# One pool of six PSUM banks in the attention stage: coarse counts move into it

## The chip, the cores and the metric

The kernel runs on one core of a Trainium2 chip. The metric is the device time of one execution in microseconds (us). TensorE (PE in the profile, its weight loads PEld), VectorE (DVE), ScalarE (ACT), GpSimd (POOL) and SyncE (SP) run side by side, each in its own order, and wait for one another through semaphores. PSUM, into which TensorE writes, has eight banks of 512 fp32 columns over 128 partitions.

## The reference, cut to what matters

```python
# attention: 8 batches, 8 heads, 576 positions, 64 wide
scores = q @ k.T / 8            # heads 0-3: the last 32 positions; heads 4-7: each fourth of the last 128
attn = exp(scores - max) / (sum + 1e-9)
x = (attn @ v) as (4608, 512)   # tokens x model width
# routing: capacity 576 tokens for each of 8 experts
logits = x @ w_gate             # (4608, 8)
for idx in argsort(-logits.flatten()):      # greedy, best pair first
    if token free and counts[expert] < 576: assign
out[tokens of e] = relu(x[tokens of e] @ w1[e]) @ w2[e]
```

## The kernel before, in words

There are two stages, attention and mixture of experts. **Attention** works in 32 units (four per batch: two kinds of head, two units each). A unit computes 36 score products into the two banks `pm` (`scores`, L398), takes masked maxima on DVE out of them (`most`, L403), subtracts them on POOL (`shift`, L409), transposes the result in three groups into banks `pS` (`turn`, L416), takes exponentials on ACT (`exps`, L412, planned at 400 ns each), multiplies by the values into banks `px` in two groups of 20 and 16 products (`values`, L424), and divides by the sums on ACT and DVE (`sums` L428, `weigh` L433 and L434). After each second unit the result is transposed in three groups into `px` (`banks`, L475) and copied out (ACT, or DVE for two of the three groups of the last units, L482). After a batch the gate's logits follow: `by_expert` and `by_token` (L516, L548), or for the last batch `narrow` (L540), whose bank is held until all parts are in; DVE copies them to `Lt` (L566).

`Router.choose` then finds for each token its best expert, key and flags (`keys` L763 to L768, `choices` L773). `coarse` compares each token's key with 256 steps (L647), one chunk of 128 tokens at a time, and `coarse_counts` (L652) counts, by two narrow products per chunk, how many tokens of each expert lie above each step. The counts of all 36 chunks add up in one bank, `pz`, which the Router owns for the whole kernel. When attention has ended, `search_alone` turns them into flags (L725), a first product (L728) and four finer rounds of comparisons and counts; the list of the first expert's tokens follows, and the experts' products, which are the second stage (`moe`).

Eight banks are given out in attention: two `pm`, two `pS`, three `px` (the third first serves as target of zero products, `keep_clock`, L119, until the 17th PE operation of the list is placed), one `pz`.

The order of instructions is written by a **planner** (`Schedule`). Each operation has an engine, an estimated cost, dependencies and a due time: the planned end less the longest path behind it, less a boost. An operation that names a `Buf` gets a bank of its pool when it is placed, the one that comes free earliest by the planner's own estimates, and the bank is held until all its users are placed. A change of the product's form on PE (`whole`, `half`, `quarter`, `narrow`) is charged. The coarse operations of the first seven batches carry a boost of -105500 ns: they are due far behind all else and go where an engine would stand idle. Once placed, each engine's order is fixed, and on the chip an engine waits for what its next instruction needs. SP issues the loads in the order in which the planner placed them.

Of the kernel before, what the change touches and what calls it, by code (L numbers as in the profile page):

```python
# [32 lines left out]
NK = 16  # L33
NM = 5
FE = 400
F0, F1 = 6, 17
PARTS = (5, 15, 16)
OB = (12, 12, 12), (6,) * 6
TOL_DVE, TOL_ACT, TOL_POOL, TOL_PE, T_W = 100, -50, 200, 500, 730
# [205 lines left out]
def attention(tc, ctx, C, load_const, T, xd, Lt, R):  # L245
# [21 lines left out]
    wgp = pk.tile([128, 4, 32], F32, name="wgp")  # L267
    LT = ring(pk, [128, S], F32, "lt", 2)
    banks_ = lambda n, k: [ps.tile([128, 512], F32, name=f"{n}{i}") for i in range(k)]
    PM, PS, PV = Pool([banks_("pm", 2)]), Pool(banks_("pS", 2)), Pool(banks_("px", 3))  # L270
    act = lambda o, i: nc.scalar.activation(o, i, AF.Copy)  # L271

    users = {}
# [182 lines left out]
    def banks(un, xs, done, usex):  # L456
# [36 lines left out]
            return  # L493
        tokens(un)

    def coarse(c0, c1, x, late):
        for c in range(c0, c1):
            g, used, use_ = PRE.take()
            f = op("DVE", 290, lambda c=c, g=g: R.coarse(c, g), [x, *used], late)
            counted[0] = op("PE", 60, lambda c=c, g=g: R.coarse_counts(c, g), [f, ready["c", 3], counted[0]], late,  # L500
                            form="whole")
            use_.append(counted[0])

    lt_ = {}

# [21 lines left out]
    def tokens(un):  # L527

        b, u = un.b, un.u
        c0, c1 = b * S // 128, (b * S + S) // 128  # L530
        late = B_K if b < B - 1 else B_E
        n = c1 - c0
        last = b == B - 1

        def narrow(gs):
            for c in range(c0, c1):
                for g in gs:
                    for p in range(0, 128, 32):
# [12 lines left out]
        if last:  # L551
            pt = Buf(PV)
            before = [*xt_[b - 1]]
            t = un.op("PE", 140 * n, lambda: narrow([0, 1]), [*before, *xt_[b][:3], ready["w"]], late, pt, "narrow")
            t = un.op("PE", 140 * n, lambda: narrow([2, 3]), [t, *xt_[b]], late, None, "narrow")
            for of in (b - 1, b):
                for kk in range(2):
                    xt_[of, kk][2].append(t)
        else:
            by_expert(un, late)  # L560
            pt = Buf(PV)
            of = [lt_[x] for x in (b - 1, b) if x >= 0]
            t = un.op("PE", 125 * n, by_token, [*(k for x in of for k in x[1]), ready["c", 3]], late, pt, "half")
            for x in of:
                x[2].append(t)
        k = un.op("DVE", 150, lambda: nc.vector.tensor_copy(  # L566
            Lt[:, c0:c1], pt.tile[:, :NE * n].rearrange("p (c e) -> p c e", e=NE)), [t], late)
        pt.users.append(k)
        x = un.op("DVE", 1000, lambda: R.choose(c0, c1), [k], late)
        coarse(c0, c1, x, B_P if not last else late - u * P_U)  # L570


    counted = [None]
    fill, warm = PV.tiles[2], R.zero
    PV.held[2] = Buf(PV)
    keep_clock(nc, warm, fill, F0)
    cold = [True]

    def idle(x, gap):
        if x.eng == "PE" and cold[0]:  # L580
            if x in PV.held[2].users:
                cold[0] = False
            elif x.n > first_pe[0]:
                keep_clock(nc, warm, fill, int(max(0, gap - 400) / 430))

    op("DVE", 300, lambda: nc.vector.memset(R.pz[:, :256], 0.0), (), B_P)
    load(0, 0, 0)
    const(0)
    const(1)
# [20 lines left out]
        Unit(u).build()  # L610
    pe = [x for x in K.ops if x.eng == "PE"]
    first_pe = [pe[0].n]
    PV.held[2].users.append(pe[F1])
    K.run(idle)


class Router:


    def __init__(self, tc, ctx, C, Lt):  # L620
        nc = tc.nc
        self.tc, self.C = tc, C
        self.pf = ctx.enter_context(tc.tile_pool(name="r_fix", bufs=1))
        self.Lt = Lt
        self.A = self.pf.tile([128, NCH], F32, name="A")
        self.PR = self.pf.tile([128, 32], F32, name="PR")
        self.M = self.pf.tile([128, NCH], F32, name="M")
        self.V0 = self.pf.tile([128, NCH], F32, name="V0")
        self.oh0 = self.pf.tile([128, NCH, NE], BF, name="oh0")
        self.key0 = self.pf.tile([128, NCH], I32, name="key0")  # L630
        self.bits = self.pf.tile([128, NCH], I32, name="bits")
        self.bt = self.pf.tile([128, 5, NE], F32, name="bt")
        self.zero = self.pf.tile([128, 512], BF, name="zero")
        self.pz = ctx.enter_context(tc.tile_pool(name="r_ps", bufs=1, space=PSUM)).tile([128, 512], F32, name="pz")
        self.open = self.pf.tile([128, NE], F32, name="open")
        nc.vector.memset(self.zero, 0.0)
        nc.gpsimd.memset(self.open, 1.0)
        nc.gpsimd.memset(self.A, 0.0)
        nc.gpsimd.memset(self.PR, 0.0)

    def work(self, ctx):
# [7 lines left out]
    def coarse_counts(self, c, g):  # L649
        nc = self.tc.nc  # L650
        for h in range(2):
            nc.tensor.matmul(self.pz[:, 400 + NE * h:400 + NE * h + NE], g[:, 128 * h:128 * h + 128], self.oh0[:, c],  # L652
                             start=(c == 0 and h == 0), stop=(c == NCH - 1), skip_group_check=True)

    def counts(self):

# [60 lines left out]
    def search_alone(self, V, oh, last):  # L717
# [1 line left out]
        nc, C, pw = self.tc.nc, self.C, self.pw  # L719
        psc = self.pa[:, :1]  # L720
        if not last:
            junk = pw.tile([128, 2, NE], F32, name="junkc")
            flag = pw.tile([128, 2], BF, name="flagc")
            for h in range(2):
                nc.vector.tensor_scalar(junk[:, h], self.pz[:, 400 + NE * h:400 + NE * h + NE], float(CAP), None,  # L725
                                        op0=OP.is_ge, op1=OP.max, accum_out=flag[:, h:h + 1])
            for h in range(2):
                nc.tensor.matmul(psc, C["unit1"], flag[:, h:h + 1], start=(h == 0), stop=(h == 1))  # L728
# [31 lines left out]
    def keys(self, c0, c1, M, key, V):  # L760

        nc = self.tc.nc
        nc.vector.tensor_reduce(M, self.Lt[:, c0:c1], axis=AX.X, op=OP.max)  # L763
# [7 lines left out]
    def choices(self, c0, c1, M, oh):  # L771

        self.tc.nc.vector.tensor_tensor(oh, self.Lt[:, c0:c1], M[:, :, None].to_broadcast([128, c1 - c0, NE]),  # L773
                                        op=OP.is_equal)

    def choose(self, c0, c1):

        sl = slice(c0, c1)
        self.keys(c0, c1, self.M[:, sl], self.key0[:, sl], self.V0[:, sl])
        self.choices(c0, c1, self.M[:, sl], self.oh0[:, sl])  # L780
        if c1 < NCH:
            self.marks(c0, c1)

# [136 lines left out]
    def close(self):  # L920
# [6 lines left out]
        self.keys(0, NCH, self.M, key, self.V)  # L927

    def ranks(self):
        nc, C = self.tc.nc, self.C  # L930
# [33 lines left out]
    def leave(self):  # L964

        nc, pw = self.tc.nc, self.pw
        Mo = pw.tile([128, NCH], F32, name="Mo")
        self.oh = pw.tile([128, NCH, NE], BF, name="oh")
        self.assign()
        nc.vector.scalar_tensor_tensor(Mo, self.A, -3e38, self.M, op0=OP.mult, op1=OP.add)  # L970
        self.choices(0, NCH, Mo, self.oh)

    def start(self):
        self.flags(self.V, None, self.kstep(0, False))
# [66 lines left out]
def moe(tc, ctx, C, R, xd, w1, w2, out):  # L1041
    nc = tc.nc
    ps = ctx.enter_context(tc.tile_pool(name="m_ps", bufs=1, space=PSUM))
    pw = ctx.enter_context(tc.tile_pool(name="m_w", bufs=1))
    R.work(ctx)
    ctx.enter_context(tc.manual_schedule())
    NF, ND = FF // 128, DM // 128
    CUT = (0, 256, CAP)
# [15 lines left out]
    HB = ring(pw, [128, 2 * CAP + 64], F32R, "hb", NF + 1)  # L1064
    Y = ring(pw, [128, DM], F32, "y", 3)
    R.pa, fill = PYR.tiles[1], PHR[0].tiles[1]


    R.alone()
# [401 lines left out]
```

## Time and profile before

| | us |
|---|---|
| median of 3 runs | 652.55 (651.42 to 652.75) |
| profiled execution | 648.04 |
| span in its trace (first to last instruction) | 646.20 |
| attention proper, tail, routing (see below) | 10 to 150, 150 to 160, 160 to 190 |

The profiled execution is 1.84 us longer than its span. Where the profile gives an instruction's duration, a run of matmuls in one line is `xN`; a matmul's end is modelled, so distances from start to start are the surer reading. Lines are those of the kernel before. The brackets at the end of a line of the timeline tell how long the engine stood idle before and what ended that.

### The profile page before, as it was taken

What the parts mean: (1) busy time and instruction counts of PE and PEld (TensorE: products, weight loads), DVE (VectorE), ACT (ScalarE), POOL (GpSimd) and SP (SyncE); (2) the same over time, 40 slices, a digit from 0 to 9 for tenths busy, and PEclk for the clock granted to TensorE, in tenths of its full rate; (3) what the DMA queues carried; (4) which work ended last, traced back from release to release, by engine and by line L of the source; (5) the groups of instructions that cost most, each with busy time, mean ns of one, the idle gap of its engine ahead of it and who ended that gap; (6) DMA issues with size and microseconds to landing.
All of it is one profiled execution on the core that took longest, in us unless ns stands there. A gap on an engine that the chain in (4) does not pass through costs nothing.

```text
span 646.2 us, 17963 instructions
## 1 busy us (share of the span) xinstructions
PE 615.7 (95%) x6749; PEld 530.2 (82%) x6749; DVE 451.1 (70%) x1930; ACT 304.8 (47%) x691; POOL 195.4 (30%) x326
## 2 busy tenths in 40 slices
PE   8999999997569999999999999999999999999994
PEld 5887888786439978977998898799889879989983
DVE  3768678875787888994998699699879736615200
ACT  3868788753037345853453425345343345325210
POOL 3434433331053156544006103400610520431011
PEclk9999999998569999999999999999999999999998
DMA  8999999823049468991155217115423743211010
GB/s 318 391 294 281 308 281 291 224 61 75 3 141 255 73 162 289 196 317 57 58 182 156 69 40 256 71 49 182 154 69 107 245 164 127 70 54 58 1 42 32
DMA packets 62680, 100.18 MB, mean 155 GB/s; under 512 B 7280, under 2 KB 26224, under 8 KB 62592
## 3 DMA queue, kind: packets, MB, share of 16 engines
q1 hardware_dynamic: 53216, 73.82, 35.4%
q0 software_dynamic: 9376, 25.21, 14.8%
q8 instruction: 53, 0.87, 0.5%
q14 instruction: 35, 0.29, 0.1%
HBM read 73.83 MB, written 18.87 MB: 143 GB/s over the span
## 4 chain that ended last, share of the span: by engine, by line
PE 75%; issue 11%; DVE 5%; POOL 2%; DMA 2%; ACT 2%; SPq 1%; POOLq 0%; DVEq 0%; ACTq 0%
PE ph L1285 26%; PE py L1327 19%; PE px L424 5%; PE pS L416 5%; PE pm L398 5%; PE px L475 2%; PE pz L660 2%; PE py L1330 2%; PE py L1332 2%; POOL out L1353 1%; DMA raw<-in_moe_w 1%; PE ph L1254 1%; PE px L516 1%; ACT vo L271 1%; PE ph L119 1%
## 5 line engine op out<-in xcount | busy, mean ns | idle before, releaser
L1327 PE MATMUL py<-w2h,hb 128*128 128x512 f32 x512 | 164.7, 394 | 0.0
L1285 PE MATMUL ph<-xh,w1h 128*128 128x256 f32 (+1 forms) x512 | 138.6, 301 | 0.0
L1285 PE MATMUL ph<-xh,w1l 128*128 128x256 f32 (+1 forms) x512 | 136.4, 297 | 0.0
L1285 PE MATMUL ph<-xl,w1h 128*128 128x256 f32 (+1 forms) x512 | 135.9, 296 | 0.0
L1327 PEld LDWEIGHTS py<-w2h,hb 128*128 128x128 f32 x512 | 96.1, 188 | 19.8
L1071 ACT ACTIVATE hb<-ph 128x256 fp32r<-128x256 f32 (+2 forms) x192 | 59.8, 346 | 105.4 <-PE ph L1285 101.6
L1327 PE MATMUL py<-w2l,hb 128*128 128x512 f32 x256 | 99.8, 390 | 0.0
L1285 PEld LDWEIGHTS ph<-xh,w1h 128*128 128x128 f32 x512 | 91.5, 189 | 0.7 <-issue 0.3
L1285 PEld LDWEIGHTS ph<-xl,w1h 128*128 128x128 f32 x512 | 91.5, 189 | 0.1
L1285 PEld LDWEIGHTS ph<-xh,w1l 128*128 128x128 f32 x512 | 91.5, 190 | 0.0
L1353 POOL DMA_INDIRECT out<-y,tok x40 | 40.2, 1006 | 147.0 <-ACT y L1071 67.4
L409 POOL TENSOR_TENSOR sc<-sc,mx 128x480 f32<-128x480 f32 x64 | 56.9, 910 | 89.6 <-DVE mx L403 89.6
L1071 ACT ACTIVATE y<-py 128x512 f32<-128x512 f32 (+1 forms) x40 | 23.9, 597 | 126.8 <-PE py L1327 100.5
L1305 DVE SCALAR_TENSOR_TENSOR hb<-ph,hb 128x320 fp32r<-128x320 f32 (+1 forms) x128 | 57.3, 452 | 28.8 <-ACT hb L1071 27.7
L403 DVE CUSTOM_DVE_ANT_0 sc<-pm,const 128x96 f32<-128x96 f32 x288 | 53.8, 253 | 22.6 <-PE pm L398 19.9
L1199 POOL DMA_INDIRECT xg<-xd,idx x40 | 42.6, 1066 | 53.3 <-issue 34.9
L1327 PEld LDWEIGHTS py<-w2l,hb 128*128 128x128 f32 x256 | 48.1, 188 | 9.1
L412 ACT ACTIVATE et<-pS 96x384 f32<-96x384 f32 x96 | 43.2, 485 | 24.4 <-PE pS L416 23.8
L1072 DVE TENSOR_TENSOR w2l<-raw,w2h 128x512 fp32r<-128x512 f32 x48 | 31.5, 684 | 20.2 <-ACT w2h L1071 19.9
L416 PE MATMUL pS<-const,sc 128*96 128x128 f32 x288 | 43.9, 281 | 0.9 <-ACT et L412 0.9
L1071 ACT ACTIVATE w1h<-raw 128x512 fp32r<-128x512 f32 x64 | 37.6, 627 | 6.6 <-DMA raw<-in_moe_w 6.6
L398 PE MATMUL pm<-k,q 64*64 64x96 f32 x1152 | 36.9, 257 | 1.8 <-DVE mx L403 0.6
(188 smaller groups left out, 982.3 us busy)
## 6 DMA issues: line engine op xcount, KB each, us to landing
raw<-in_moe_w SPq DMA_DIRECT2D x128, 256.0 KB, 4.5
k<-in_kp SPq DMA_DIRECT2D x16, 304.0 KB, 6.1
k<-in_kd SPq DMA_DIRECT2D x16, 304.0 KB, 6.3
q<-in_qp SPq DMA_DIRECT2D x16, 288.0 KB, 5.4
q<-in_qd SPq DMA_DIRECT2D x16, 288.0 KB, 6.3
xd<-xs SPq DMA_DIRECT2D x64, 72.0 KB, 3.2
xd<-xs SPq DMA_DIRECT2D x16, 288.0 KB, 6.7
w2l<-raw POOLq DMA_DIRECT2D x16, 256.0 KB, 5.2
```

What stands on the lines that cost most here:

```text
L398: nc.tensor.matmul(o[w:w + 64], self.Q[c][r:r + 64], self.K[c][r:r + 64], start=True, stop=True)
L403: nc.vector.tensor_tensor_reduce(out=sc[:, c], in0=pms[g][:, c // 2 * KB:c // 2 * KB + KB], in1=mm[:, c if self.kind else min(1, c)], scal ...
L409: nc.gpsimd.tensor_tensor(sc[:, g::2], sc[:, g::2], mx[:, g::2, None].to_broadcast([128, n, KB]), op=OP.subtract)
L412: nc.scalar.activation(self.E0[:, 384 * j:384 * j + 384], pt[:KB, :384], AF.Exp, scale=-1.0)
L416: nc.tensor.transpose(pt[:KB, 128 * x:128 * x + 128], sc[:, ORD[3 * j + x]], C["identf"])
L424: nc.tensor.matmul(px[64 * a:64 * a + 64, x - c0], self.E0[:, w:w + 64], self.V[c][a], start=True, stop=True)
L1071: act = lambda o, i, f=AF.Copy: nc.scalar.activation(o, i, f)
L1199: nc.gpsimd.indirect_dma_start(out=xg[:n], out_offset=None, in_=xd, in_offset=bass.IndirectOffsetOnAxis(ap=box[0][:n, m:m + 1], axis=0))
L1285: nc.tensor.matmul(o, a[:, d * 128:d * 128 + 128], b[:, d, c0:c1], start=((d, i) == pairs[0]), stop=((d, i) == pairs[-1]))
L1305: hl = op("DVE", 335 if j == 0 else 400, lambda: nc.vector.scalar_tensor_tensor(hb[:, CAP + c0:CAP + c1], o, 0.0, hb[:, c0:c1], op0=OP.max ...
L1327: nc.tensor.matmul(py, x, w, start=(f + i == 0), stop=(f == NF - 1 and i == 2))
L1353: s = nc.gpsimd.indirect_dma_start(out=out, out_offset=bass.IndirectOffsetOnAxis(ap=box[1][:n, m:m + 1], axis=0), in_=y[:n], in_offset=None)
```

## The change

- `pS`, `px` and the Router's `pz` give up their own banks: attention now has two `pm` banks and one pool of six (`PV`, also named `PS`). The sixth serves the zero products at first, until the same 17th PE operation.
- Coarse counts of a batch take a bank of that pool. For the first seven batches all chunks of a batch are one PE operation, which starts the bank anew, and a DVE addition (`coarse_sum`) adds the 16 columns to a table `cc` in SBUF. For the last batch, an identity product first puts `cc` into the bank (`coarse_sum_of`), the chunks' counts add to it one by one as before, and DVE reads the flags out of it at once (`coarse_flags`); `search_alone` uses these.
- In the last batch `choose` reads the logits out of their bank, and ACT copies them to `Lt` beside it; in the other batches DVE copies them first, as before.
- `pz` is taken from the second stage's banks; its zeroing moves from DVE at the start to ACT at the beginning of the second stage.
- One more zero product at the start: seven in place of six.

```diff
-F0, F1 = 6, 17
+F0, F1 = 7, 17
-    PM, PS, PV = Pool([banks_("pm", 2)]), Pool(banks_("pS", 2)), Pool(banks_("px", 3))
+    PM, PV = Pool([banks_("pm", 2)]), Pool(banks_("px", 6))
+    PS = PV
...
     def coarse(c0, c1, x, late):
+        gs, pt, last = [], Buf(PV), c1 == NCH
         for c in range(c0, c1):
             g, used, use_ = PRE.take()
             f = op("DVE", 290, lambda c=c, g=g: R.coarse(c, g), [x, *used], late)
-            counted[0] = op("PE", 60, lambda c=c, g=g: R.coarse_counts(c, g), [f, ready["c", 3], counted[0]], late,
-                            form="whole")
-            use_.append(counted[0])
+            gs.append((c, g, f, use_))
+        k = None
+        if last:
+            k = op("PE", 60, lambda: R.coarse_sum_of(pt.tile), summed[-1:], late, buf=pt, form="whole")
+        for part in [[y] for y in gs] if last else [gs]:
+            def count(part=part):
+                for c, g, *_ in part:
+                    R.coarse_counts(c, g, pt.tile, c == c0 and not last, c == c1 - 1)
+
+            k = op("PE", 10 + 50 * len(part), count, [*(y[2] for y in part), ready["c", 3], k], late,
+                   buf=None if k else pt, form="whole")
+            for y in part:
+                y[3].append(k)
+        f = R.coarse_flags if last else R.coarse_sum
+        summed.append(op("DVE", 200, lambda: f(pt.tile), [k], late))
+        pt.users.append(summed[-1])
...
-        k = un.op("DVE", 150, lambda: nc.vector.tensor_copy(
-            Lt[:, c0:c1], pt.tile[:, :NE * n].rearrange("p (c e) -> p c e", e=NE)), [t], late)
-        pt.users.append(k)
-        x = un.op("DVE", 1000, lambda: R.choose(c0, c1), [k], late)
+        if last:
+            x = un.op("DVE", 1000, lambda: R.choose(of_bank(pt), c0, c1), [t], late)
+            pt.users += [x, un.op("ACT", 250, keep, [t], late)]
+        else:
+            k = un.op("DVE", 150, keep, [t], late)
+            pt.users.append(k)
+            x = un.op("DVE", 1000, lambda: R.choose(Lt[:, c0:c1], c0, c1), [k], late)
         coarse(c0, c1, x, B_P if not last else late - u * P_U)
...
-    op("DVE", 300, lambda: nc.vector.memset(R.pz[:, :256], 0.0), (), B_P)
...
+    def coarse_sum(self, pt):
+        o = self.cc.rearrange("p h e -> p (h e)")
+        self.tc.nc.vector.tensor_tensor(o, o, pt[:, :2 * NE], op=OP.add)
+    def coarse_sum_of(self, pt):
+        self.tc.nc.tensor.matmul(pt[:, :2 * NE], self.C["identf"], self.cc.rearrange("p h e -> p (h e)"), start=True,
+                                 stop=False, skip_group_check=True)
+    def coarse_flags(self, pt):
+        for h in range(2):
+            self.tc.nc.vector.tensor_scalar(self.cj[:, h], pt[:, NE * h:NE * h + NE], float(CAP), None,
+                                            op0=OP.is_ge, op1=OP.max, accum_out=self.cf[:, h:h + 1])
...
+    nc.scalar.activation(R.pz[:, :256], R.zero[:, :256], AF.Copy)
```

## Rows read from the trace of the kernel before

**Rows 1.** The page: TensorE's share, and its granted clock in 40 slices

```profile
PE 615.7 (95%) x6749; PEld 530.2 (82%) x6749; DVE 451.1 (70%) x1930; ACT 304.8 (47%) x691; POOL 195.4 (30%) x326
...
PEclk9999999998569999999999999999999999999998
```

**Rows 2.** Stretches: length, then busy us of each engine, clock, DMA share, GB/s

```profile
10.00:150.00 140.00, 137.46 (x2966) 113.40 (x2964) 105.57 (x764) 106.34 (x244) 55.14 (x62) 1.00 0.86 268
150.00:160.00 10.00, 6.38 (x159) 5.08 (x158) 4.94 (x20) 2.55 (x8) 0.00 (x0) 0.87 0.28 62
160.00:190.00 30.00, 17.80 (x276) 11.49 (x277) 23.62 (x97) 3.44 (x6) 6.26 (x9) 0.53 0.17 51
```

**Rows 3.** Waits of TensorE, 9 to 150 us: total us, times, longest us

```profile
PE pS L416 <- ACT et L412: 0.6, 2, 0.4
PE pm L398 <- DVE mx L403: 0.6, 2, 0.3
```

**Rows 4.** The chain that ended last, 15 to 25 us: start, us, what

```profile
17.46 1.20 PE px L424 x36
...
19.53 0.73 PE px L424 x20
...
22.15 0.62 PE px L424 x16
```

**Rows 5.** Timeline of the tail: start, us, engine, line, operation [idle before]

```profile
147.95 0.86 PE L540 MATMUL px<-wgp,xt 128*32 128x8 f32 x80
...
151.62 0.87 ACT L412 ACTIVATE et<-pS 96x384 f32<-96x384 f32 x2 [0.43 <-PE pS L416]
...
152.16 0.53 PE L416 MATMUL pS<-const,sc 128*96 128x128 f32 x3 [0.31 <-ACT et L412]
...
152.62 0.80 PE L424 MATMUL px<-v,et 96*64 96x65 f32 x20
...
155.22 0.84 PE L475 MATMUL px<-const,xs 128*128 128x128 f32 x6 [1.33 <-DVE xs L434]
155.78 1.02 DVE L482 COPY xt<-px 128x384 f32<-128x384 f32 x2 [0.70 <-PE px L475]
...
156.39 0.55 PE L475 MATMUL px<-const,xs 128*128 128x128 f32 x3 [0.32 <-DVE xt L482]
...
156.98 0.49 ACT L271 ACTIVATE xt<-px 128x384 f32<-128x384 f32 x1 [2.86 <-PE px L475]
...
158.81 0.20 DVE L566 COPY Lt<-px 128x40 f32<-128x40 f32 x1 [2.00 <-PE px L540]
159.04 0.20 DVE L763 TENSOR_REDUCE M<-Lt 128x5 f32<-128x40 f32 x1
...
160.22 1.00 PE L652 MATMUL pz<-oh,pre 128*128 128x8 bf16 x10 [1.46 <-DVE pre L647]
...
179.85 0.60 ACT L992 ACTIVATE rx<-oa,const 128x360 bf16<-128x360 bf16 x1 [22.38 <-DVE oa L983]
```

**Rows 6.** Timeline: first and last counts before the tail; an addition out of PSUM

```profile
63.43 0.20 PE L652 MATMUL pz<-oh,pre 128*128 128x8 bf16 x2
...
150.89 0.26 PE L652 MATMUL pz<-oh,pre 128*128 128x8 bf16 x4
...
183.67 0.17 DVE L1013 TENSOR_TENSOR t<-t,ptx 64x20 f32<-64x20 f32 x1
```

**Rows 7.** Timeline of TensorE in the first 14 us

```profile
1.20 2.74 PE L119 MATMUL px<-zero 128*128 128x512 bf16 x6 [1.20 <-DVE zero L636]
4.48 1.86 PE L398 MATMUL pm<-k,q 64*64 64x96 f32 x36 [0.54 <-DMA k<-in_kp]
...
7.74 1.95 PE L398 MATMUL pm<-k,q 64*64 64x96 f32 x36
...
12.72 1.04 PE L398 MATMUL pm<-k,q 64*64 64x96 f32 x36
```

**Rows 8.** Groups by line, 0 to 158 us: count, busy us, mean ns, idle before

```profile
L412 ACT ACTIVATE et<-pS 96x384 f32<-96x384 f32 x96 | 43.2, 485 | 24.4 <-PE pS L416 23.8
```

More of the change, by code (lines that the diff above doesn't have):

```diff
@@ L494, in banks @@
         tokens(un)
+    summed = []
     def coarse(c0, c1, x, late):
+        gs, pt, last = [], Buf(PV), c1 == NCH
         for c in range(c0, c1):
@@ L565, in tokens, with keep, of_bank @@
                 x[2].append(t)
-        k = un.op("DVE", 150, lambda: nc.vector.tensor_copy(
-            Lt[:, c0:c1], pt.tile[:, :NE * n].rearrange("p (c e) -> p c e", e=NE)), [t], late)
-        pt.users.append(k)
-        x = un.op("DVE", 1000, lambda: R.choose(c0, c1), [k], late)
+        def keep():
+            (act if last else nc.vector.tensor_copy)(Lt[:, c0:c1], of_bank(pt))
+        def of_bank(pt):
+            return pt.tile[:, :NE * n].rearrange("p (c e) -> p c e", e=NE)
+        if last:
[5 more added lines that the diff above has]
+            x = un.op("DVE", 1000, lambda: R.choose(Lt[:, c0:c1], c0, c1), [k], late)
         coarse(c0, c1, x, B_P if not last else late - u * P_U)
-    counted = [None]
-    fill, warm = PV.tiles[2], R.zero
-    PV.held[2] = Buf(PV)
+    fill, warm = PV.tiles[5], R.zero
+    PV.held[5] = Buf(PV)
     keep_clock(nc, warm, fill, F0)
@@ L580, in idle @@
         if x.eng == "PE" and cold[0]:
-            if x in PV.held[2].users:
+            if x in PV.held[5].users:
                 cold[0] = False
@@ L612, in attention @@
     first_pe = [pe[0].n]
-    PV.held[2].users.append(pe[F1])
+    PV.held[5].users.append(pe[F1])
     K.run(idle)
@@ L633, in __init__ @@
         self.zero = self.pf.tile([128, 512], BF, name="zero")
-        self.pz = ctx.enter_context(tc.tile_pool(name="r_ps", bufs=1, space=PSUM)).tile([128, 512], F32, name="pz")
+        self.cc, self.cj = (self.pf.tile([128, 2, NE], F32, name="c" + x) for x in "cj")
+        self.cf = self.pf.tile([128, 2], BF, name="cf")
         self.open = self.pf.tile([128, NE], F32, name="open")
@@ L638, in __init__, with work @@
         nc.gpsimd.memset(self.A, 0.0)
+        nc.gpsimd.memset(self.cc, 0.0)
         nc.gpsimd.memset(self.PR, 0.0)
-    def work(self, ctx):
+    def work(self, ctx, ps):
+        self.pz = ps.tile([128, 512], F32, name="pz")
         self.pw = ctx.enter_context(self.tc.tile_pool(name="r_work", bufs=2))
@@ L647, in coarse, with coarse_counts @@
         self.tc.nc.vector.tensor_scalar(g, self.C["coarse"], self.V0[:, c:c + 1], None, op0=OP.is_le)
-    def coarse_counts(self, c, g):
-        nc = self.tc.nc
+    def coarse_counts(self, c, g, pt, start, stop):
         for h in range(2):
-            nc.tensor.matmul(self.pz[:, 400 + NE * h:400 + NE * h + NE], g[:, 128 * h:128 * h + 128], self.oh0[:, c],
-                             start=(c == 0 and h == 0), stop=(c == NCH - 1), skip_group_check=True)
+            self.tc.nc.tensor.matmul(pt[:, NE * h:NE * h + NE], g[:, 128 * h:128 * h + 128], self.oh0[:, c],
+                                     start=(start and h == 0), stop=stop, skip_group_check=True)
+    def coarse_sum(self, pt):
[8 more added lines that the diff above has]
+                                            op0=OP.is_ge, op1=OP.max, accum_out=self.cf[:, h:h + 1])
     def counts(self):
@@ L721, in search_alone @@
         if not last:
-            junk = pw.tile([128, 2, NE], F32, name="junkc")
-            flag = pw.tile([128, 2], BF, name="flagc")
             for h in range(2):
[L725 to L728, printed above, removed]
+                nc.tensor.matmul(psc, C["unit1"], self.cf[:, h:h + 1], start=(h == 0), stop=(h == 1))
         base = kb = None
@@ L758, in search_alone, with keys @@
         self.delta = psc
-    def keys(self, c0, c1, M, key, V):
+    def keys(self, L, M, key, V):
         nc = self.tc.nc
-        nc.vector.tensor_reduce(M, self.Lt[:, c0:c1], axis=AX.X, op=OP.max)
+        nc.vector.tensor_reduce(M, L, axis=AX.X, op=OP.max)
         bits = M.bitcast(I32)
@@ L769, in keys, with choices, choose @@
         self.lo = halves[:, :, 0]
[L771 to L776, printed above, removed]
+    def choices(self, L, M, oh):
+        self.tc.nc.vector.tensor_tensor(oh, L, M[:, :, None].to_broadcast([128, L.shape[1], NE]), op=OP.is_equal)
+    def choose(self, L, c0, c1):
         sl = slice(c0, c1)
-        self.keys(c0, c1, self.M[:, sl], self.key0[:, sl], self.V0[:, sl])
-        self.choices(c0, c1, self.M[:, sl], self.oh0[:, sl])
+        self.keys(L, self.M[:, sl], self.key0[:, sl], self.V0[:, sl])
+        self.choices(L, self.M[:, sl], self.oh0[:, sl])
         if c1 < NCH:
@@ L926, in close @@
         self.V, key = pw.tile([128, NCH], F32, name="V"), pw.tile([128, NCH], I32, name="key")
-        self.keys(0, NCH, self.M, key, self.V)
+        self.keys(Lt, self.M, key, self.V)
     def ranks(self):
@@ L970, in leave @@
         nc.vector.scalar_tensor_tensor(Mo, self.A, -3e38, self.M, op0=OP.mult, op1=OP.add)
-        self.choices(0, NCH, Mo, self.oh)
+        self.choices(self.Lt, Mo, self.oh)
     def start(self):
@@ L1044, in moe @@
     pw = ctx.enter_context(tc.tile_pool(name="m_w", bufs=1))
-    R.work(ctx)
+    R.work(ctx, ps)
     ctx.enter_context(tc.manual_schedule())
```

## The prediction

> **What bounds the kernel now.** I read the page first. TensorE is busy 95% of the span and its granted clock is full except in one dip [rows 1], so I look for where it is not the bound. The table by stretch (busy time of each engine) separates three parts: attention proper from 10 to 150 us, where PE is busy 137.46 of 140.00 us; the tail of attention from 150 to 160 us, 6.38 of 10.00; and routing from 160 to 190 us, 17.80 of 30.00 at a granted clock of 0.53 [rows 2]. All edits lie in the first two parts and in the first 5 us. The experts, from 190 us on, keep their code, so I let them only move earlier or later as a whole.
>
> In attention proper TensorE has 140.00 - 137.46 = 2.5 us of idle time, and that is the most that better order can recover from idling there. The list of waits says how much of it is a wait for a PSUM bank: the transposes of the scores waited 0.6 us in two places for ScalarE's exponentials to empty a bank of the pair pS [rows 3]. A second sort of loss is hidden in busy time. In the chain of waits, 36 value products in one piece take 1.20 us, but split as 20 and 16, with other work between, 0.73 + 0.62 = 1.35 us [rows 4]: 0.15 us for two more changes of the kind of product, about 0.075 each. That is the price of being unable to finish a group in one go.
>
> In the tail TensorE waits for a chain of single steps through DVE and ACT, and there every removed step counts in full [rows 5].
>
> **The change part by part.** *The copy of the last logits.* Before, the last product ends, DVE copies 40 logits at 158.81, and the search for the largest starts at 159.04 [rows 5]. After, it reads the bank itself, so 159.04 - 158.81 = 0.23 us leaves the path. Two DVE instructions (the maximum and the choices) then read PSUM in place of SBUF. The copy from PSUM took 0.20 us and the maximum from SBUF, of the same shape, 0.20 too [rows 5], so I price this at 0 to 0.05 us. Gain 0.2. The ACT copy that fills Lt has an idle engine: ACT next worked 22.38 us after its last attention instruction [rows 5], and Lt is read again only by the first closing of an expert, long after.
>
> *The third transpose of the last units.* Two of the three px banks are used at 155.22; the narrow product before them has held the third, its logits not being complete. So the third group of transposes starts at 156.39, after 0.32 us in wait of a DVE copy, and then an ACT copy and the narrow product follow it in series [rows 5]. With six banks, one with the logits and at most one with counts, it needn't wait: 0.32 us gained. The other branch, DVE's two copies, would end at 155.78 + 1.02 = 156.80, still ahead of ACT's at 156.98 + 0.49 - 0.32 = 157.15, so the branch that is shortened stays the longer one.
>
> *The third turn of the last unit.* It waited 0.31 us for a bank of pS [rows 5]. Its follower, the values, needs just the first two turns' exponentials, which were there 0.1 us before they were used, so only 0.1 of it shows. The tail thus gives 0.2 + 0.3 + 0.1 = 0.6 us.
>
> *The counts in the pool.* The same 72 narrow products run, now in one group per batch, except in the last. They came in small groups: two took 0.20 us and four 0.26, with what follows overlapping. Up to 158 us, 62 of them lie in 14 such groups, of which the first and the last stand in [rows 6]; seven groups would save at most seven times 0.075, so I take 0.3. The group waits for all four or five masks of a batch, and whatever stands behind it on PE waits too; since its due time is far behind all others it is placed in gaps. Each batch but the last adds one DVE addition of 128x16 out of PSUM. Nearest row: an addition of 128x20 with one operand in PSUM, 0.17 us [rows 6]. Seven make 1.2 us, on an engine that is busy 105.57 of 140.00 us [rows 2]; they go in idle time, so 0, and up to 1.2 if each delayed a score stage (which waits behind it on DVE, and the next scores with it). In the tail DVE is idle long enough. One more product, which puts the earlier sum into the last bank, has PE idle 1.46 us before the last counts [rows 5]: 0. The two flag instructions keep their place in DVE's order: 0.
>
> *Banks in the middle.* I recover the 0.6 us of bank waits [rows 3], and with the 0.3 of the counts the middle gives 0.9. Upper end: all 2.5 us of idle time and 0.9 of splits, of which I count six at 0.15. Lower end: a loss, the rival on the other side below.
>
> *The first 5 us.* Six zero products take 2.74 us and TensorE is then idle 0.54 us, until the first keys land [rows 7]. A seventh takes at most 2.74 / 6 = 0.46 us and so ends before the first scores, 0.54 us later: 0. If the load came sooner it would cost at most 0.46. The zeroing on DVE that goes stood ahead of the first maxima, which wait for the first scores anyway; its successor on ACT lies in the long ACT idle time: 0. SP's loads and GpSimd's order are not moved by hand; their due times may shift with the rest.
>
> **The sum.** Tail 0.6 and middle 0.9: 1.5 us. The profiled execution took 648.04 us: a span of 646.20 and 1.84 around it; it would become 646.5. The median of the three runs, 652.55, is 4.5 us above that execution, and I take the same 1.5 off it: 651.05, rounded to **651.0 us**. Some 0.2%, 1.3 us, is what a measurement of this kernel can tell from no change, so even the expected result stands close to that edge.
>
> **The rivals.** *Banks are not what the middle waits for* (651.95). TensorE was idle in 1.8% of the middle, and a wait that goes can come back at the next product, which needs the same POOL or ACT result. For it: the waits for DVE's maxima are as long as those for banks, 0.6 us [rows 3]. Then only the tail's 0.6 remains: 651.95.
>
> *An earlier full clock* (648.5). The first 36 scores took 1.86 us, the next 1.95, and the third group 1.04 [rows 7], so TensorE ran at the lower of its levels, 1.2 GHz, at first, though the granted clock of the first slice reads full [rows 1]. What came before the rise is 0.54 us of idle time inside the first work. If the seventh product lets the clock rise one group earlier, the second scores save 1.95 - 1.04 = 0.9 us, and what hangs on them through DVE, POOL and PE starts earlier by as much. With all of the middle's idle time as well: 0.6 + 2.5 + 0.9 = 4.0, thus 648.5. Against it: this start is bound by the DVE maxima and the loads as much as by PE. By the Trainium skill, "TensorE: Matmul & The Clock Gate", section "What's actually happening", the slow level is the default and activity releases it; the trace agrees as far as that the slow products stand at the start and after the routing's idle time, and no row shows what a filled gap does.
>
> *The copy doesn't leave the path* (652.15). ACT's copy of Lt and DVE's maximum want one bank at the same moment, 158.81. If they're kept apart and ACT's stands first, a copy of 0.2 us stands ahead of the maximum as before; with nothing gained in the middle 0.6 - 0.2 = 0.4 us is left: 652.15. For it: the other pair of readers of one bank, ACT's sums and DVE's weighing, runs in that order everywhere, by a dependency of its own. The Trainium skill, "PSUM — Partial Sum Buffer", section "PSUM bank collisions raise a hardware error", says that two engines may not touch one bank in the same partitions at once, reads with reads included; the trace before has no such pair without a dependency, so no row shows it.
>
> *Slower: the shared pool lets turns take the banks of values* (654.7). The planner counts an exponential as 400 ns and it takes 485 [rows 8], so a bank that it believes free is not, and the in-order PE stands still. In two separate pools such an error hits only turns; in one pool the values and logits inherit it. The price is one wait of the tail's kind, 0.31 us [rows 5]. At twelve of them (fewer than one in two units) 3.7 us is lost against 1.5 gained: 652.55 + 2.2 = 654.7. It decides, beyond what can be measured, from nine waits on (1.5 + 1.3 over 0.31). Against it: six banks are one more than the five they replace, and ACT is busy 106.34 of 140.00 us in the middle [rows 2], so late exponentials catch up.
>
> **How the numbers follow.** Forecast, gains of 0.9 to 2.5 us: 0.48, two thirds of it (0.32) beyond 1.3 us. Banks don't matter: 0.15. Earlier clock: 0.16. Copy on the path: 0.09. Slower: 0.12. Faster by over 0.2%: 0.32 + 0.16 = 0.48; within 0.2%: 0.16 + 0.15 + 0.09 = 0.40; slower: 0.12. The range reaches to the earlier clock's 648.5 and, on the other side, to nine waits of the slower case, 652.55 + 1.3 = 653.85: 648.4 to 653.8. Outside lie half of the earlier clock's chance and most of the slower case, together under 0.2.
>
> **What would show it.** In the profile after: the maximum at the first DVE place after the last narrow product, with no 128x40 copy ahead of it; the third transposes of the tail without a wait for DVE; no wait of the turns for the exponentials in the middle; counts in groups of eight and ten; the second scores in 1.95 us again, or in about 1.0, which decides on the clock; and a start of the routing search about 1.5 us earlier. I am wrong if attention gets longer by waits of values or logits for ACT, if the changes of kind grow in number, or if the difference lies after 190 us, where I count nothing.

## The result: 7.0 us faster, and the profile after

The changed kernel takes 645.63 us (median of 6 runs, 644.39 to 648.06) against 652.65 us before (6 runs, 651.42 to 657.81): a ratio of 0.988, 95% interval 0.984 to 0.992, or 7.0 us. 651.0 us was forecast, with a range from 648.4 to 653.8. The direction was right, the size was not: about 1.5 us had been expected. Executions over 1.5% above the fastest of their kernel are left out of the comparisons, here and below, unless all runs are given.

The page of the profile after, beside [rows 1]: TensorE's busy time falls by 5 us, at nearly the same granted clock, and its share of the span stays what it was.

```profile
span 643.0 us, 17974 instructions
PE 610.7 (95%) x6753; PEld 531.2 (83%) x6753; DVE 451.3 (70%) x1935; ACT 304.3 (47%) x693; POOL 196.4 (31%) x327
PEclk9999999996589998999999999999999999999998
```

The profiled execution took 644.78 us with a span of 643.0, so this pair of profiles shows only 3.2 us of the 7.0. The reason lies behind attention. The last product of attention ends at 158.76 us before (it starts what [rows 5] show from 158.81 on) and at 151.84 after, 6.9 us earlier. From there to the end of the span it is 487.4 us before, 491.2 after, and 490 to 495 in the four other whole kernels below, whose code there is the same: the profiled execution of before, 648.04, was quicker than all six timed beside the result (651.42 to 657.81). Eleven runs of that kernel on another chip took 646.42 to 649.12; what made the profiled one quick stays open. So the time of that last product is the cleaner measure of a profile, and it agrees with the medians.

TensorE from the first scores to that last product, before and after (columns as in [rows 2]):

```profile
4.40:158.80 154.40, 149.36 (x3197) 122.32 (x3197) 111.39 (x793) 108.89 (x252) 56.91 (x64) 1.00 0.83 259
```

```profile
4.40:152.00 147.60, 142.53 (x3200) 121.58 (x3200) 112.18 (x800) 107.51 (x253) 57.08 (x64) 1.00 0.85 270
```

This pair holds the surprise. Idle time is 154.40 - 149.36 = 5.0 us before and 147.60 - 142.53 = 5.1 after: none was gained. The same products (three more) take 149.36 - 142.53 = 6.8 us less *busy* time, at a granted clock that reads 1.00 in both. In the shorter pair of kernels measured below, idle time falls from 7.1 to 6.3 us and busy time by 5.8, so there too the gain is nearly all busy time.

By kind of product, with consecutive instructions of one form taken together as a run and measured from its start to the next start, less the idle time that is shown, the busy time is

| us | before | after |
|---|---|---|
| transposes and counts | 58.9 | 55.5 |
| values and logits by token | 43.6 | 41.9 |
| scores | 34.8 | 33.1 |
| zero products and the rest | 12.0 | 12.1 |

Of the 1.8 us of the scores, 0.9 is one group: the second scores, which ran slowly before (1.95 us [rows 7]) and in 1.04 after, as told under the start below. The 5.1 us of the first two kinds have two causes. First, there are fewer runs. A unit's scores are turned by nine transposes. Before, 9 of the 47 runs with such turns hold exactly nine, 28 six and 9 three; after, 27 of 34 hold nine, 3 six and 3 three. Runs of the first two kinds together fall from 91 to 69 up to the last product. Second, some of the time called busy is waiting. These are instructions of before; the two groups of 20 values are the same work:

```profile
27.79 1.07 ACT L271 ACTIVATE vo<-v 64x1040 f32<-64x1040 f32 x1
...
28.77 0.47 ACT L271 ACTIVATE xt<-px 128x384 f32<-128x384 f32 x1
29.10 1.04 PE L424 MATMUL px<-v,et 96*64 96x65 f32 x20
29.14 0.84 ACT L412 ACTIVATE et<-pS 96x384 f32<-96x384 f32 x2
...
32.77 0.80 PE L424 MATMUL px<-v,et 96*64 96x65 f32 x20
```

At 29.10 they take 1.04 us (0.82 to the start of the next values), while ACT gets to the rest of their exponentials only at 29.14, after two copies; at 32.77 they take 0.80 (0.63). No wait is shown for the difference, 0.2 us: instructions that come one by one, as their operands get ready, are grouped and called busy.

The chain that ended last in the profile after (start, us, what) shows whole groups:

```profile
22.61 0.79 PE px L417 x6
23.41 1.20 PE px L425 x36
24.61 0.97 PE pm L399 x36
25.58 1.12 PE px L417 x9
```

Six transposes take 0.79 us and nine 1.12, so one takes (1.12 - 0.79) / 3 = 0.11 and a run costs 0.79 - 6 x 0.11 = 0.13 beside them. A least-squares fit of such runs of ten traces (18 to 142 us; runs that deviate by over 0.15 us left out; the rest scatters by 0.02) gives about 0.11 per transpose, 0.03 per value product and 0.14 us (0.145 in the expectations below) for each run of transposes or of values. 22 runs fewer are then 3.1 us; at the 0.08 that inserted products show below, 1.8. What is left of the 5.1 us, 2.0 to 3.3, is by this count hidden waiting. What the fit leaves over agrees with the lower figure: it falls from 3.6 us before to 1.5 after.

### The profile page after: what moved, and what is told of

Read it like the earlier page. It is cut to its first block, busy times and chain, and to the rows that moved or that the text cites. A ratio compares the mean times of both kernels' runs of the same rounds, so it can differ in the third digit from the quotient of the medians.

```text
span 643.0 us, 17974 instructions
## 1 busy us (share of the span) xinstructions
PE 610.7 (95%) x6753; PEld 531.2 (83%) x6753; DVE 451.3 (70%) x1935; ACT 304.3 (47%) x693; POOL 196.4 (31%) x327
## 4 chain that ended last, share of the span: by engine, by line
PE 75%; issue 12%; DVE 6%; POOL 3%; DMA 2%; ACT 1%; SPq 0%; POOLq 0%; DVEq 0%
PE ph L1322 27%; PE py L1364 19%; PE px L425 5%; PE px L417 5%; PE pm L399 5%; PE pz L702 2%; PE px L476 2%; PE py L1367 2%; PE py L1369 2%; POOL out L1390 1%; PE ph L1291 1%; PE px L533 1%; DVE sc L404 1%; DMA raw<-in_moe_w 1%; DMA k<-in_kp 1%
## 5 line engine op out<-in xcount | busy, mean ns | idle before, releaser
L413 ACT ACTIVATE et<-px 96x384 f32<-96x384 f32 x96 | 40.7, 484 | 22.4 <-PE px L417 20.8
L417 PE MATMUL px<-const,sc 128*96 128x128 f32 x288 | 39.1, 278 | 1.0 <-DVE xs L435 0.7
L399 PE MATMUL pm<-k,q 64*64 64x96 f32 x1152 | 35.3, 252 | 2.0 <-DMA k<-in_kp 1.3
```

The costliest lines, as they stand in the source:

```text
L399: nc.tensor.matmul(o[w:w + 64], self.Q[c][r:r + 64], self.K[c][r:r + 64], start=True, stop=True)
L413: nc.scalar.activation(self.E0[:, 384 * j:384 * j + 384], pt[:KB, :384], AF.Exp, scale=-1.0)
L417: nc.tensor.transpose(pt[:KB, 128 * x:128 * x + 128], sc[:, ORD[3 * j + x]], C["identf"])
```

## Experiments: which part of the change brings it

Theories. *Shared banks*: the turns may use any bank, so a unit's three turns and its values go in whole groups. *A fourth bank for values*: the sixth bank alone shortens waits, with the two pools kept. *Grouped counts*, *the seventh zero product* and *the last copy* are the rest of the change. Each edit of the banks also makes the planner write another order of instructions; what the banks are worth in an unchanged order wasn't tried.

**Two pools, one with four banks.** The change with the turns kept on two banks of their own; four banks for values and counts.

```diff
-    PM, PV = Pool([banks_("pm", 2)]), Pool(banks_("px", 6))
-    PS = PV
+    PM, PS, PV = Pool([banks_("pm", 2)]), Pool(banks_("pS", 2)), Pool(banks_("px", 4))
```

> The changed kernel, but its six banks stay divided, two for the turns and four for values, transposes, logits and counts. Planned changes of the product's form in attention: 138, against 137 before and 114 in the changed kernel. Theory 'fewer changes of form' (each costs TensorE about 0.25 us, from 5.9 us of busy time over 22 pieces in the two traces): the middle's gain is gone, the last product of attention ends at about 157.5 to 158.5 us (before 158.8, changed 151.9), and the time is 650 to 652. Rival 'the sixth bank': what counts is one bank more than before, not the sharing; then it stays near the changed kernel, 646 to 647. Rival 'earlier clock': it has the seventh zero product, so at least 1 us better than before.

**One pool, nothing else.** The kernel before with its two turn banks and three value banks in one pool of five; counts keep `pz`.

```diff
-    PM, PS, PV = Pool([banks_("pm", 2)]), Pool(banks_("pS", 2)), Pool(banks_("px", 3))
+    PM, PV = Pool([banks_("pm", 2)]), Pool(banks_("px", 5))
+    PS = PV
```

> The kernel before, with the five banks of turns and values in one pool and nothing else changed (counts in their own bank, six zero products). Planned changes of form: 114. Theory 'fewer changes of form': nearly the whole gain, 23 changes at 0.25 = 5.8 us, so 646.5 to 648 and an end of attention near 153 us. Rival 'the sixth bank': little, 651 to 652.5. Rival 'grouped counts' or 'earlier clock': little as well, since neither is in it.

**Grouped counts, nothing else.** The kernel before, with a batch's counts as one operation (but for the last batch).

```diff
+        for part in [[y] for y in gs] if c1 == NCH else [gs]:
+            counted[0] = op("PE", 10 + 50 * len(part), lambda part=part: [R.coarse_counts(y[0], y[1]) for y in part],
```

> The kernel before, with the counts of a batch as one operation on TensorE (still in the Router's own bank, added up there). Planned changes of form: 128, nine fewer. Theory 'fewer changes of form': 9 times 0.25 = 2.2 us, so 650 to 651. Rival 'grouped counts': most of the 7 us, 646 to 648. If changes of form cost only the 0.075 us of the prediction, 0.7 us: 652.

**The change again**, beside these.

> The changed kernel once more, for comparison on the same chip: 644.5 to 647, about 7 us under the kernel before, with the end of attention near 152 us. It also shows whether the second scores run in 1.0 us and whether they wait for the keys again.

Measured on one chip, where the kernel before took 653.23 us (13 runs):

| | us | ratio (95%) | last product of attention |
|---|---|---|---|
| two pools, 2 and 4 | 647.55 | 0.990 (0.985 to 0.994) | 155.46 |
| one pool of five | 646.12 | 0.988 (0.983 to 0.992) | 152.47 |
| grouped counts | 652.01 | 0.998 (0.995 to 1.001) | 157.21 |
| the change | 644.94 | 0.985 (0.981 to 0.990) | 155.28 |

One pool alone brings what the change brings, within what is measured. Its runs of transposes and values number 70 up to the last product, and 27 of them hold whole groups of nine turns. But the theory of shared banks was missed at the other end: with two pools it expected most of the gain to be lost, and a fourth value bank without sharing brings 5.7 us. The grouped counts alone gain 1.2 us in the medians, where the theory of shared banks, which priced a run at 0.25 us, expected 2 to 3, and none is not excluded. The last row's 155.28 stands out and is followed up below.

**The same in a shorter kernel.** Four kernels were then cut behind the routing search, to measure tenths without the 450 us of the experts: these and nearly all of the output are left out. The other kernels from here on are cut in the same way.

```diff
+    y = Y.tiles[0]
+    nc.vector.tensor_copy(y[:, :2 * NCH], R.pre.rearrange("p w c -> p (w c)"))
+    nc.sync.dma_start(out[:128, :2 * NCH], y[:, :2 * NCH])
+    return
```

> The kernel before, cut after the search for the first expert: the experts' products and nearly all of the output are left out, so that attention and search stand alone without the experts' scatter (in six traces the time after attention was between 487 and 495 us). In the trace of before the search's last step ends at 178.1 us; with the store of one small tile and what lies around the span about 182 to 185 us. This is the base for the three others.

> The changed kernel, cut in the same way. Theory 'fewer changes of form' (114 planned against 137, 0.25 us each, and about 1 us in the tail and the start): 6 to 7.5 us under the cut kernel before. If the gain came from the experts' stage instead, nothing here.

> The changed kernel with its six banks divided two and four (138 changes of form), cut in the same way. The whole kernel gave 647.55 us, 5.7 under before, where the theory of form changes expected 1 to 2. Theory 'fewer changes of form': 1 to 2.5 us under the cut kernel before (tail, start, the last copy). Rival 'the sixth bank': 4 to 6 us under it, near the cut changed kernel.

> The kernel before with five banks in one pool (114 changes), nothing else changed, cut in the same way. Theory 'fewer changes of form': 5 to 6.5 us under the cut kernel before, within 1.5 us of the cut changed kernel. Rival 'the sixth bank': 0 to 2 us under it.

| cut kernel | us (runs kept, of all) | last product | runs of transposes and values up to it |
|---|---|---|---|
| before | 182.2 (4 of 6) | 158.2 | 91 |
| the change | 176.39 (5 of 5) | 151.59 | 69 |
| two pools, 2 and 4 | 178.08 (5 of 5) | 153.43 | 94 |
| one pool of five | 175.04 (3 of 6) | 152.99 | 70 |

All six runs of one pool of five took 174.2 to 181.0, with a median of 176.29; its profile is that of a run of 177.09.

The change brings 5.8 us here, so nearly all of its 7.0 lies ahead of the experts. Two pools bring 4.1 us with three *more* runs than before, as the rival of the fourth bank expected (4 to 6) and not the theory (1 to 2.5). Fewer runs can't be the cause there; that it is shorter waiting, hidden or shown, for a bank of values is likely but not separated from the seventh zero product, the grouped counts and the tail, which this kernel has too. Going on from two pools to six shared banks removes 25 runs and is worth 1.7 us (95% interval -0.2 to 3.1). At 0.145 each it would be 3.6, at the 0.08 measured next 2.0. How the 7 us divide between runs and waits is therefore known only roughly.

**The price of a change of form, by itself.** Into the changed kernel, cut, 32 tiny products are put, one behind the first transpose of each unit (the trace shows each as two instructions): once with 64 output rows, which is another form and makes two runs more, once with 128, which is the same form.

```diff
             for x in range(3):
+                if x == 1 and j == 0:
+                    nc.tensor.matmul(pt[:64, 400:408], C["identf"][:, :64], C["identf"][:, :8], start=True, stop=True)
```

> The changed kernel, cut after the search (no experts, nearly no output), once more as the base for the three others of this job: 175.5 to 177.5 us, as before (176.39).

> The cut changed kernel with one small product of the values' form (64 output rows) put between the first and second transpose of each of the 32 units: it ends a run of transposes and begins a new one, so 64 more changes of form. A fit of 755 pieces of ten traces gives 0.145 us to each run of transposes and to each run of value products, whatever its length, beside 0.108 per transpose and 0.029 per value product. By it: 32 times (2 x 0.145 + about 0.03) = 10.2 us over the base, 186 to 188. By the prediction's 0.075 per change: 32 times (0.15 + 0.03) = 5.8 us, 182. If changes of form cost nothing: 1 us.

> The same with a small product of the transposes' own form (128 output rows) in the same place, which changes no form: the control. The fit gives one transpose of 128 columns 0.108 us; with 8 columns, bound by its weights' load, 0.06 to 0.11: 2 to 3.5 us over the base.

Two places of the timeline, first the half form, then the whole one:

```profile
62.26 0.31 PE L419 MATMUL px<-const,sc 128*96 128x128 f32 x1
62.50 0.28 PE L418 MATMUL px<-const 128*64 128x8 f32 x2
62.72 1.08 PE L419 MATMUL px<-const,sc 128*96 128x128 f32 x8
```

```profile
59.82 0.32 PE L419 MATMUL px<-const,sc 128*96 128x128 f32 x1
59.97 0.29 PE L418 MATMUL px<-const 128*128 128x8 f32 x2
60.11 1.06 PE L419 MATMUL px<-const,sc 128*96 128x128 f32 x8
```

Start to start, the half form takes 0.24 + 0.22 us for what the whole form does in 0.15 + 0.14: 0.17 us for two runs more, 0.085 each. All 32 places show it: 0.42 to 0.46 us with the half form, 0.25 to 0.29 with the whole one. Over the stage the last product comes at 160.13 against 154.86 (base: 151.99), 5.3 us for 64 runs, 0.08 each. The times differ by less (184.93 against 182.21 us, medians of four; the whole form spreads from 179 to 184, its profile is the quickest, and the half form's 184.99; base 176.20): 2.7 us or 0.04 each. The half form was expected at 186 to 188 by the fit and at 182 by the prediction's price, and came between; the whole form cost 6.0 us over the base in its median and 2.9 in its quickest run, where 2 to 3.5 were expected. So a run has a price of its own whatever the order, 0.08 us in these traces. The fit's 0.14 is higher, and waits that stand at the start of a run would be in it; whether that is the reason isn't shown. 22 runs are 1.8 to 3.1 us.

**Five shared banks, counts among them.** The change without its sixth bank.

```diff
-    PM, PV = Pool([banks_("pm", 2)]), Pool(banks_("px", 6))
+    PM, PV = Pool([banks_("pm", 2)]), Pool(banks_("px", 6)[:5])
```

> The cut changed kernel with five banks in the shared pool, the sixth unused (117 changes of form planned, against 114). If sharing does it: within 1 us of the base. If a sixth bank is worth what the two divided pools gained (4.5 us under the cut kernel before without fewer changes): 3 to 5 us over the base.

It took 179.2 to 184.0 us in seven runs (base 176.20; an eighth, twice as long, is left out), 3 us or more over the base, where sharing alone should have kept it within 1; the last product ends at 154.92. The timeline shows one place, where the next batch's counts stand in TensorE's order behind the addition that has to empty their bank:

```profile
128.12 0.41 PE L678 MATMUL px<-oh,pre 128*128 128x8 bf16 x10 [2.12 <-DVE cc L684]
128.42 2.13 PE L417 MATMUL px<-const,sc 128*96 128x128 f32 x9
```

The counts in the pool are no gain by themselves: they need the bank that `pz` gave up. The nine turns after the wait took 2.13 us in place of 1.12; the granted clock is 0.80 from 125 to 130 us and 0.86 from 130 to 135. One pool of five that leaves the counts in `pz`, above, has no such wait.

**Small parts.** In the changed, cut kernel: six zero products; the copy of the last logits on DVE ahead of the choice, as before; a charge for a change of form in the planner of 6000 in place of 3000. In the cut kernel before: grouped counts.

```diff
-F0, F1 = 7, 17
+F0, F1 = 6, 17
```

> The cut changed kernel (no experts; base 176.2 to 176.4 us) with six zero products at the start in place of seven. Theory 'the banks do it': within 0.5 us of the base, since the second scores of the changed kernel wait for keys or maxima (1.26, 0.97 and 1.53 us of idle time in three traces) and not for the clock. Rival 'earlier clock': 0.9 us slower or more, 177.2 or above, with second scores in 1.8 to 1.95 us as in the profile of before.

```diff
-            (act if last else nc.vector.tensor_copy)(Lt[:, c0:c1], of_bank(pt))
+            nc.vector.tensor_copy(Lt[:, c0:c1], of_bank(pt))
-        if last:
+        if False:
```

> The cut changed kernel with DVE's copy of the last logits back on the path and the search reading Lt in SBUF. By the prediction 0.2 us slower. In the trace after, the search started 0.28 us after the last product, ACT's copy first, where before it started 0.27 us after it behind DVE's copy: so no difference beyond 0.1 us is expected now, 176.2 to 176.5.

```diff
-TURN, T_TURN = 3000, 95
+TURN, T_TURN = 6000, 95
```

> The cut changed kernel with the planner's penalty for a change of form at 6000 ns in place of 3000 (TURN): 61 runs of transposes and values planned in place of 70, banks as in the changed kernel. At 0.145 us each 1.3 us under the base, 174.9 to 175.1. If the gain of the change is banks alone: no difference. If the loads of values are the next bound (ACT waited for them 0.3 to 4.9 us in traces of the changed kernel, never in those of before): less than 0.7.

> The cut kernel before (base 182.56) with the counts of a batch as one operation, in their own bank: 83 planned runs in place of 92. At 0.145 us each 1.3 us under the base, 181.3. The whole kernel gave 1.2 us. If grouping were most of what the two divided pools gained: 178 to 179.

| cut kernel | us (runs kept, of all) | against |
|---|---|---|
| six zeros | 177.59 (5 of 6) | the change: +1.2 (-0.7 to 2.1) |
| copy first | 176.24 (5 of 6) | the change: -0.1 (-2.0 to 1.3) |
| charge 6000 | 175.4 to 181.2, all six runs | the change, all five: 175.8 to 178.3 |
| grouped counts | 181.70 (5 of 6) | before: -0.5 (-1.4 to 0.6) |

The four ran on another chip than the kernels that they are set against; the cut change took 176.39 and 176.20 on two. The copy is worth nothing, as expected of it. The seventh zero product and the grouped counts are each worth about a microsecond or less and can't be told from nothing. The 177.59 of six zeros lies where the rival of the earlier clock expected it (177.2 or above), but its profile doesn't bear that out: the second scores take 1.33 us, and the third start at 12.99, among the 12.30 to 13.32 of five profiles with seven zero products. The higher charge gives 61 runs in place of 69 and not the 174.9 to 175.1 expected of them: its profiled execution (180.3 us) has a wait of 2.4 us at 127 us. That is the place where the repeated change lost time too, and it is told next.

**The new weak place.** In the repeated change (the whole kernel, last product at 155.28) the timeline has

```profile
121.70 0.83 SPq L313 DMA_DIRECT2D v<-in_vd  x2
...
127.31 1.07 ACT L272 ACTIVATE vo<-v 64x1040 f32<-64x1040 f32 x1 [4.39 <-DMA v<-in_vd]
128.28 1.22 ACT L413 ACTIVATE et<-px 96x384 f32<-96x384 f32 x3
128.81 1.35 PE L425 MATMUL px<-v,et 96*64 96x65 f32 x20 [2.61 <-ACT et L413]
```

and its table by stretch

```profile
125.00:130.00 5.00, 2.39 (x61) 2.05 (x60) 2.68 (x21) 2.67 (x5) 0.99 (x1) 0.83 0.83 221
130.00:135.00 5.00, 5.00 (x62) 4.15 (x62) 3.08 (x17) 2.91 (x7) 0.83 (x1) 0.50 0.21 40
```

ACT stands for 4.39 us at a copy of values that haven't landed; the exponentials are queued behind it, and TensorE waits 2.61 us for them. Then it works at a granted clock of 0.50. SP issued that load at 121.70, behind stores of results, against 117.98 in the first profile of the change, which has no such wait. ACT's waits for `in_vd` between 9 and 150 us sum to 0.3 to 4.9 us in nine of the twelve kernels that are the change or made from it, and to nothing in the other three; of the six that are the kernel before or made from it, only one has any (0.9 us). So most of the faster kernels meet loads that were early enough before. Speed alone isn't the reason: one pool of five is as fast, has no such wait in either form, and in its cut form issued the load at 121.50, but its ACT came to the copy only at 126.37. Why the load was issued late in some executions stays open, and it wasn't tried to issue these loads earlier.

## Why the prediction was wrong

**The bound of the middle.** "The most that better order can recover from idling there" was 2.5 us: right as a sentence, since the idle time didn't shrink, and wrong as a bound on the gain, since what went was busy time. This is the step that failed: the middle was given 0.9 us, and as its upper end the idle time and 0.9 of splits. I read 137.46 of 140.00 us busy [rows 2] as work. The products need less: over the whole stage the same work takes 6.8 us less of it after. The parts were in view in rows that I used: 36 values in 1.20 us or in 0.73 + 0.62 [rows 4].

**The term of splits.** The price of 0.15 us per split, two more runs at 0.075, was right by the inserted products (0.17) and half of what the fit gives (0.28). The number was wrong: six splits were taken as an upper end, where 22 runs, eleven splits, disappeared. The two turn banks hold two of a unit's three groups, so nearly every unit had to split (28 runs with six turns, 9 with nine); that could have been counted in the trace before.

**The bank waits of the middle**, 0.6 us, went, but another came. After, no turn waits for an exponential, among the waits of TensorE from 9 to 150 us; one turn waits 0.7 us for DVE's weighing `xs`, which it doesn't read (its operand comes from GpSimd), so most likely for a bank of values that it now shares.

```profile
PE pm L399 <- DMA k<-in_kp: 1.3, 1, 1.3
PE px L476 <- DVE xs L435: 0.9, 1, 0.9
PE px L417 <- DVE xs L435: 0.7, 1, 0.7
PE px L678 <- DVE cc L684: 0.4, 1, 0.4
```

So this term brought nothing in idle time, as the rival that banks are not what the middle waits for had it. The waiting that went stood in busy time, 2.0 to 3.3 us by the count above.

**The tail.** Forecast 0.6. From the start of the last transposes to the search for the largest it is 159.04 - 155.22 = 3.82 us before [rows 5] and 152.12 - 148.81 = 3.31 after, a gain of 0.5:

```profile
148.81 1.20 PE L476 MATMUL px<-const,xs 128*128 128x128 f32 x9 [0.92 <-DVE xs L435]
149.40 1.02 DVE L483 COPY xt<-px 128x384 f32<-128x384 f32 x2 [0.64 <-PE px L476]
...
150.59 1.24 PE L557 MATMUL px<-wgp,xt 128*32 128x8 f32 x76 [0.41 <-ACT xt L272]
151.88 0.20 ACT L272 ACTIVATE Lt<-px 128x40 f32<-128x40 f32 x1 [1.34 <-PE px L557]
152.12 0.20 DVE L800 TENSOR_REDUCE M<-px 128x5 f32<-128x40 f32 x1 [1.70 <-ACT Lt L272]
```

All nine transposes go in one run, without the wait, as forecast, and this brings the whole 0.5 and not 0.3. The copy brings nothing: ACT's copy and DVE's maximum read one bank, ACT's comes first and the trace gives it as what DVE waited for. The maximum starts 152.12 - 151.84 = 0.28 us after the product's end, against 159.04 - 158.76 = 0.28 before. So the mechanism of the rival that the copy doesn't leave the path was true, and copying first on DVE costs nothing either. The Trainium skill, "PSUM — Partial Sum Buffer", section "PSUM bank collisions raise a hardware error", forbids two engines one bank in the same partitions at once; here the two reads, 151.88 and 152.12, stand one behind the other, and no run shows whether they could overlap.

**The start.** Forecast 0.

```profile
1.20 3.17 PE L119 MATMUL px<-zero 128*128 128x512 bf16 x7 [1.20 <-DVE zero L661]
4.43 1.86 PE L399 MATMUL pm<-k,q 64*64 64x96 f32 x36
6.23 1.28 PE L119 MATMUL px<-zero 128*128 128x512 bf16 x3
8.77 1.04 PE L399 MATMUL pm<-k,q 64*64 64x96 f32 x36 [1.26 <-DMA k<-in_kp]
...
13.32 1.04 PE L399 MATMUL pm<-k,q 64*64 64x96 f32 x36
```

The rival of the earlier clock got its row: the second scores take 1.04 us, not 1.95 [rows 7]; with six zero products they took 1.33. But they start at 8.77, after 1.26 us in wait of keys, where they started at 7.74, and the turns behind them start at 9.75 against 9.61. The third scores start at 13.32 against 12.72, with six more turns ahead of them. So 0.9 us of busy time went and came back as waiting, and 0 was nearly right. One pool of five, uncut, has six zero products, second scores of 1.80 us and the whole gain. The rival's time (648.5) lay nearest to the result by luck, for another reason than its own.

**The counts and the slower rival.** The additions and the one more product cost 0.4 us in one wait, the last of the list above; grouping is worth anything from nothing to 1.2, and 0.3 was forecast. That late users of a bank hold up others is real, 2.1 us at once with five banks, but with six it stayed at that one wait and the turn's 0.7.

**The edge of what can be told.** 0.2%, 1.3 us, was thought to be enough to tell a result from no change; the interval of the result reaches 2.4 us to either side.

## What to carry to other kernels

Busy time of an in-order engine isn't work: compare the shortest time that a group takes with what the same group takes elsewhere, and count the groups, before the idle time is taken as what order can win. Where a group needs three banks, a pool of two splits it nearly every time; pooling the same number of banks among their users cost nothing here and brought 7 of 653 us. And after such a gain, look for the waits for loads anew: nine of the twelve kernels with the change had one.

## What the runs showed of the hardware

A change between transposes (128 rows out) and products with 64 rows out costs 0.08 us on TensorE, even with all operands ready and other work queued, as the 32 inserted products show; a fit over runs of ten traces gives 0.14. And three waits of TensorE amid full work were followed by a fall of the granted clock: from 130 to 135 us it was 0.86 after the 2.12 us wait, 0.54 after the 2.4 us wait of the higher charge, and 0.50, the lower of its two levels (1.2 GHz), after the 2.61 us wait. After a wait of 1.09 us near the same place in the cut change it was 1.00. So such a wait can cost more than its length: where the load was late, the last product came 155.28 - 151.84 = 3.4 us later than in the first profile of the change, though not all of this is shown to be that wait's.
